# The first k, v and q of a linear-attention and ReGLU kernel: half of k, all of v and q by head halves on Pool's DMA queue, in a new order

## The chip, the cores and the metric

One core of a Trainium2 chip runs the kernel. The metric is the device time of one execution in microseconds (us); the times of several runs are given by their median. Engines are named as in the profile: PE (TensorE), DVE (VectorE), ACT (ScalarE), POOL (GpSimd) and SP (SyncE, which only issues DMAs here).

## What is computed

The reference has two parts. The first is attention with a feature map, for 8 batches of 8 heads, 576 positions and head size 64; the second is a gated feed-forward network (FFN) over the 4608 tokens.

```
def phi(x):                                   # w_phi: 64 x 128
    proj = einsum('bhsd,df->bhsf', x, w_phi)
    proj = proj - max(abs(proj), axis=-1, keepdims=True)
    return concatenate([exp(proj), exp(-proj)], axis=-1)
q_p, k_p = phi(q), phi(k)
kv  = einsum('bhsf,bhsd->bhfd', k_p, v);   z = sum(k_p, axis=2)
num = einsum('bhsf,bhfd->bhsd', q_p, kv);  den = einsum('bhsf,bhf->bhs', q_p, z) + 1e-6
x   = (num / den) as 4608 x 512
out = (maximum(x @ w_gate, 0) * (x @ w_val)) @ w_out      # 512 -> 1536 -> 512
```

## The kernel before, in words

**Stages of a batch.** The first 512 positions of each head are laid on 128 partitions in four chunks; the last 64 of each head ("the rest", km, vm, qm) are worked on two heads at a time. k comes in as kn, is turned to kT (PE with an identity matrix for batches 0 and 1, DMA transposes on SP after that, L310 to L342), is multiplied by w_phi on PE (`rows`, L389), and DVE takes the row maxima (L400) while ACT takes two exponentials of each bank (L350). The maxima are put into v: `scale` (L415, L422) makes vs from vn, on Pool for most heads and on DVE for the last pair of heads of batch 0. `k_kv` (L482) sums kv on PE, and ACT or DVE copies it out. q is turned to qT, projected (L506) and exponentiated; its maxima come from L516, in batch 0 from L562 and L569. `q_num` (L600) multiplies by kv; DVE combines the two signs into t and u (L608, L615), takes the reciprocal r (L625), and Pool divides (L628) into xu, which is turned to xT: on PE for batches 0 and 1 (L641, L648), by DMA on SP later.

**FFN.** For each group of 512 tokens (group g is batch g's main part, a ninth group is all the rests) and each of 12 column blocks: four matmuls with wv (L669), ACT's copy to val (L675), four with wg (L669), and DVE's product to h (L678). Then 12 matmuls with wo (L707) for each of four row blocks, a copy (L718) and a store on SP. Group 0 is cut into three parts of 128, 128 and 256 columns, so that the first can start when chunk 0 of xT is there; the others are one part of 512.

**Loads of batch 0.** SP brings k in four loads of two heads each, 256 KB, in f32 (`kn32`), into memory that later holds w_out, k's rest behind it (`km32`), then v in four loads and v's rest. Two gates (L775, L785) put later loads behind k: the first gated load on SP waits for k's last part, and q's first load on Pool for the third of the four. q comes on Pool in two loads of two chunks each for all heads, cast to bf16 on the way. w_phi comes on ACT's queue. Everything else (the next batches, the weights) comes on Pool's queue.

**Order.** Nothing is scheduled when the kernel is built: each operation is put down with its engine, cost and key in a plan, and ORDER (L1016) is a written-out list of all of them: the number of the operation, a letter for the engine and the slots of its buffers and banks. `w` and `z` entries are warm-up matmuls on a tile of zeros (L199), 120 of them. Each engine runs its own in the order of the list and waits at the first whose inputs are missing. The costs in the plan (2.4 for the identity, 1.25 for a turn by DMA, 0.5 for a store) do not reach the program. From batch 2 on the code keeps turns by DMA and Pool's loads apart: a turn waits for the last load on Pool to land, a load for the last turn.

Of the kernel before, what the change touches and what calls it, by code (L numbers as in the profile page):

```python
# [15 lines left out]
PE, ACT, DVE, POOL, SP = "PE", "ACT", "DVE", "POOL", "SP"  # L16
# [84 lines left out]
def kernel(  # L101
# [12 lines left out]
    B, H, S, D = q.shape  # L114
# [4 lines left out]
    C = 4  # L119
# [85 lines left out]
    def buf(name):  # L205
        return Buf(R[name])
# [9 lines left out]
    o_ident = op(POOL, 2.4, setup, key=(0, 1))  # L216
# [118 lines left out]
    def turn_dma(src, dst, nbytes, dst_buf, deps, key, src_buf, pad=0.0):  # L335
        def go():
            return nc.sync.dma_start_transpose(out=dst(), in_=src())

        o = op(SP, 1.25, go, deps, [src_buf, dst_buf], key=key, kind="a", nbytes=nbytes,
               pad=pad)  # L340
        o.alone = True
        return o  # L342
# [210 lines left out]
    def q_scale_rows(cp, qT, turned, key):  # L553
# [3 lines left out]
        for i in range(NU):  # L557
# [17 lines left out]
            a = op(PE, 0.22, rows, [turned[cp], o_w, o_wz], [qT], [ps], key, "a")  # L575
# [79 lines left out]
    def ffn(g, xb, parts, o_wv, o_wg, o_wo):  # L655
# [38 lines left out]
        for t in range(4):  # L694
            for lo, hi in ((0, DM),) if g < B or t < 3 else ((0, DM // 2), (DM // 2, DM)):
# [32 lines left out]
                if g < B:  # L728
                    op(SP, 0.5, store, [c_], [ob], key=(1, g), kind="l", nbytes=P * DM * 4)
# [17 lines left out]
    for b in range(B):  # L747
        ins[b] = {n: buf(n) for n in ("kn", "qn", "vn", "km", "vm") if b or n[0] != "k"}
        if b % 2 == 1:
            ins[b]["qm"] = buf("qm")  # L750
# [3 lines left out]
    kn32 = k32[:, 0 : H * C * D].rearrange("p (h c d) -> p h c d", h=H, c=C)  # L754
    km32 = k32[:, H * C * D : H * C * D + NU * D].rearrange("p (j d) -> p j d", j=NU)
# [9 lines left out]
    k_heads = ((0, 2), (2, 4), (4, 6), (6, 8))  # L765
    o_km = load_rest_by_head(0, k, SP, (0, 1.5), None, (), 0.0, km32)
    got["km", 0] = o_km
    ks = []
    for i, (lo, hi) in enumerate(k_heads):
        o = load_main(0, "kn", k, SP, slice(lo, hi), (0, i), None, (), 0.0, kn32)  # L770
        ks.append(o)
        for h in range(lo, hi):
            got["kn", 0, h] = o
    heads_of(0, "vn", v, SP, 0, 2, (0, 4))
    heads_of(0, "vn", v, SP, 2, 4, (0, 5), [ks[3]]).gate = ks[3]  # L775
    got["vm", 0] = load_rest_by_head(0, v, SP, (0, 6), ins[0]["vm"])
    heads_of(0, "vn", v, SP, 4, 6, (0, 7))
    heads_of(0, "vn", v, SP, 6, 8, (0, 8))

    for cp in range(C // 2):  # L780
        o = load_main(0, "qn", q, POOL, slice(0, H), (0, 10, cp), ins[0]["qn"], [] if cp else [ks[2]], 0.0, None,
                      slice(2 * cp, 2 * cp + 2))
        if cp == 0:
            o_first = o
            o_first.gate = ks[2]  # L785
        got["qn", 0, cp] = o
# [38 lines left out]
    for b in range(B):  # L825
# [7 lines left out]
        wide = b == 0  # L833
        if wide:
            kn = km = None
            kflat = lambda: kn32.rearrange("p h c d -> p (h c d)")
            kmf = lambda: km32.rearrange("p j d -> p (j d)")
        else:
            kflat = lambda kn=kn: kn.t.rearrange("p h c d -> p (h c d)")
            kmf = lambda km=km: km.t.rearrange("p j d -> p (j d)")  # L840
        qflat = lambda qn=qn: qn.t.rearrange("p h c d -> p (h c d)")
        turned_k, tq = {}, []
        if b < TURNS:
            for u in range(NU):
                o = turn_pe(
                    lambda i, u=u, f=kflat: f()[:, P * (4 * u + i) : P * (4 * u + i + 1)],
                    lambda u=u, kT=kT: kT.t[:, 4 * u : 4 * u + 4],
                    4, kT, [got["kn", b, 2 * u]], (*ak, 0, u), kn,
# [6 lines left out]
            for x in range(2):  # L855
                if wide:
                    at, load = slice(x, None, 2), got["qn", b, x]
                else:
                    at, load = slice(8 * x, 8 * x + 8), got["qn", b, 0]
                tq.append(turn_pe(  # L860
                    lambda i, at=at, f=qflat: f().rearrange("p (n b) -> p n b", b=P)[:, at][:, i],
                    lambda at=at, qT=qT: qT.t[:, at],
                    8, qT, [load], (*ak, 0, 6, x), qn,
                ))
# [36 lines left out]
        def q_two(cp, mq, key, qT=qT, tq=tq, wide=wide):  # L901

            qps, reds, exd = (buf("qp"), buf("qp")), [], ([], [])
            for hq in range(2):
                rd, ex = q_cols(
                    hq, qT, [tq[cp if wide else hq]],
# [15 lines left out]
        if first:  # L922
            cols, scales = {}, {}
            for cp in range(C // 2):
# [3 lines left out]
                scales[cp] = q_scale_rows(cp, qT, tq, (*ak, 1, cp, 1))  # L928
# [56 lines left out]
    for g in range(B + 1):  # L985
        if g == 0:
            xT, xo = xTs[0]
            parts = [(0, P, xo[0:1]), (P, 2 * P, xo[1:2]), (2 * P, SF, xo[2:4])]
# [28 lines left out]
0G 3D 8S 4D 1S 7S 9S 15S0 6S 5G w29 35P00 10S 2D 13S0 36D w17 57P120000 33P3 16G0 59A 61D 37P4 34A  # L1017
58D 17G 63A w8 47P561111 38D 62A 41P00 26G1 51D 49A 67P342222 50A 42D 39P2 12S 22G0 68D 52A 87P0000
14S 71D 60A 11S 23G0 90A 40D 64A 72A 88D w21 77P12333 29G 73A 48D 74A 65A 89A 81D w10 43P40 91A5
75A 69A 78D 66G 83A 92D 44D 84A0 54A 70A 85D 93D w20 119P4 79A 82A 94D 76G 80A w12 108P3201 86D 53A  # L1020
115P5 97P10 110A 117P6 55A 116D0 111A 56G 45P0 98A 118D 109A 101P51 46D 112A 103P16 102A 113P3 120D
107A 136P2 18G 138P0 114D 134P5 106A 99P42 20G 104A 139D1 95P63 105A 135D 21G 122P3723 100A 137D
96A 132P0 121A0 147P10000 19G 124A 144P51 133D 141P42 127P62 125A 145D 193P01 126A 142D 146D 123A
148D 195P7 143D 201P51 140A1 194A 149D 160P31111 154P42 202D 150D 157P10 128A 161D 207P500403 151G
155D 129A 158D 156D 131A 162D 247P61110 25G1 159D 167P40222 196A 211D 173P31 170P10 130A 197P7 168D
249A 174D 152P20 171D 250A 163D 172D 164G 208D 153A 203P11 213A 248D 28G 212A z3 183P21000 169D
165P6 175D 198A 217P403534 184D 24G1 176D 204A 199P3 166D 1359P70 185D 180P62 30G 218D 1383P21
1360A 210A 1375P12 200D 1387P73 177G 209A 181D 186P31 221D 1376A 1361P5 1384A 1388A 205P1 187D 220A
1362D0 1389P2 188D 219A 178P7 182D 1377P5 1390D 223A 237P362025 189D 206D 190G 1363P40 251A 222A
1385P2 241D 1371P13 239A 1365P0 27G0 1386D 1364A 179D 1372A 191P2 242A 1378D 227P411210 1366D 243A  # L1030
192D 277P75010 1373P0 231D 31G 240A 1379P21 283A 1374D 1367P62 252D 32G 1380A 1381P0 238D 224A 232A
1391P20 1382D 253G 233A 1393P3 225D 1368A 1369P0 278D 1392A 1395P13 282A 254G 1397P6 1370D 1415P21
280A 228D 1403P02 1396A 1416A 1394D 1405P1 226G 229A 1398D 281D 1407P20 234A 1417P3 1404A 1408A
1409P6 1406D 279A 270P0523 1418D 230A 263P21 235D 1399P73 273A 1410D 1423P32 236G 274D 1447P41
1400A 1425P6 1424A 1401P7 1448A 244A 1449P3 1426D 245A 1411P40 275A 1402D 1451P62 1450D 267D 1412A
276A 1435P73 1413P3 246G 271D 1453P4 1452A 214A 265A 1419P51 1414D 259P64 1454D 1436A 272A 264D
1443P30 1437P7 260A 284P40 215A 266A 1438D 257P65 216G 285D 1420A 1444A 1445P7 288D 1431P22 258A
261P56 1432A 1446D 268A 291P30 1455P63 262D 269A 1421P2 255P77 292D 1456A 290A 293D 1422D 1427P50
294A 256D 301P10110 347P60 1428A 298P21 289A 295P32 1457P7 299D 1429P5 348A 300D 1487P01 1458D 286A
296D 311P21221 302D 287A 1433P6 303D 1439P73 1430D 1488A 1441P4 312D 1440A 313D 1471P10 383G0  # L1040
1489P0 1434D 1442D 308P50 297D 1479P72 381G1 1490D 1463P23 1480A 309D 1472A 1481P6 314P41 310D
1464A 1473P3 384G0 1482D 1459P01 349P7120 1474D 304D 1460A 1461P2 305G 353D 1467P52 1508P6 1468A
1462D 315D 382G1 316D 306P31 350D 1491P00 324P50002 1495P21 1492A 317D 1497P4 307A 318G 1465P0 355A
321P30 1509P 1466D 351A 322D 1496A 325D 354A 1475P03 326D 352A 356P20 323D 337P11111 1498D 1469P5
1476A 357D 340P32 327P70 338D 1499P41 328D 1518P0 341D 1500A 342D 358D 1470D 359A 329D 1493P4
1483P32 330D 339D 334P52 331G 1501P2 1484A 335D 319P7 336D 1477P1 1494D 369P30220 375P51 1478D
372P42 1519P 343D 320D 344G 376D 373D 1485P1 1502D 1503P7 387S0 1486D 370D 371D 345P2 332P1 374D
388S0 1504P 333A 346A 1505P 389S0 1531P30 386S 1520P 360P40 363P12 1521A0 1523P23 364D 1506A1 361D
365D 1532A 1510P 1507S 1524A 390S 431P00001 1539P71 432D 377D 1527P12 435A 434A 433A 366P32 1525P2
1540A 367D 362D 1511A2 391P501312 1526D1 1528A 401P743131 1541P6 393A 385G0 397A 392D 1513P1 403A  # L1050
1542D 406A 530G1 1535P23 395D 394A 529G1 368D 1529P6 398A 436D 407A 402D 399A 1514P 396A 400G 405D
404A 421P532524 378D 1530D 411P040200 1537P7 414A 531G1 427A 412D 1533P6 426A 413A 1515P 437G 408A
1536A 409D 1543P01 416A 425D 532G0 424A 1534D 1547P22 417A 1516D1 1544A 1545P3 422D 527G0 415D
1551P60 423A 379G 1538D 428A 418A 1549P1 1552A 1546D 438G 1548A 447P04301 454P57 1550D 468P6312
450A 1555P23 528G0 470A 472D 1567P11 469D 1556A 410G 455D 471A 1553P2 448D 1568A 453A 439P68 1554D
474A 1563P12 451D 449A 460A 380S0 1557P2 440D 429A 452A 458D 430G 461P06 1564A 441P49 1522S 465D
# [123 lines left out]
```

## Time and profile before

| what | us |
|---|---|
| median of 9 runs | 382.59 |
| lowest and highest | 381.73 and 386.31 |
| profiled execution | 380.45 |
| its span | 378.7 |
| busy: PE, DVE, ACT, POOL | 365.9, 265.1, 236.9, 169.7 |
| first matmul of the FFN starts | 30.49 |
| last copy of PE's results to SBUF starts | 373.99 |

The profile is one execution. The page lists each engine's busy time, its share of the span, and groups of instructions by line, engine and tile with their mean duration. A line of a timeline has the start, the time from the first start to the last end of the merged instructions, engine, source line, operation, tiles, and in brackets how long the engine sat idle before and what ended that. A row of waits has the engine, the line that waited, the line waited for, the sum in us, the number of times and the longest. Busy PE is not PE at its peak, and warm-up matmuls count as busy.

### The profile page before, as it was taken

To read this page: it belongs to the slowest core of one execution; us is meant where nothing else is said; L and a number is where in the kernel's file an instruction comes from. 1 tells how busy PE (TensorE), PEld (TensorE's weight loads), DVE (VectorE), ACT (ScalarE), POOL (GpSimd) and SP (SyncE) were. 2 spreads that over 40 slices of the span, in tenths; PEclk is the share of its full clock that TensorE was granted. 3 is DMA by queue.
4 is the path that set the end of the run, shared out by engine and by line. 5 is a ranking of instruction groups with operands and counts; after the bars stand their busy time and mean duration, and the time that the engine had idled before them with its cause. 6 is when DMAs were issued, how large, how long until landed. Compare 5 with 4: busy or idle time off the path is not lost.

```text
span 378.7 us, 8753 instructions
## 1 busy us (share of the span) xinstructions
PE 365.9 (97%) x3329; PEld 208.0 (55%) x3375; DVE 265.1 (70%) x650; ACT 236.9 (63%) x546; POOL 169.7 (45%) x201
## 2 busy tenths in 40 slices
PE   8889999999999999998999999999999999999994
PEld 8767897544654655455446544654465544444452
DVE  6999888478897798868866998589647636222431
ACT  4999974498779757975786589567843322214111
POOL 4788945079448732991774259621742200100000
PEclk9999999999999999999999999999999999999999
DMA  6999997759958837988548669850400400020016
GB/s 179 220 183 223 197 172 170 99 148 138 147 146 176 161 61 157 115 199 148 155 96 94 138 148 226 117 118 3 125 2 3 109 31 0 16 83 28 2 42 181
DMA packets 85609, 45.00 MB, mean 119 GB/s; under 512 B 56672, under 2 KB 79072, under 8 KB 85568
## 3 DMA queue, kind: packets, MB, share of 16 engines
q0 software_dynamic: 32800, 21.83, 35.4%
q1 hardware_dynamic: 52448, 22.42, 26.2%
q8 instruction: 26, 0.43, 0.5%
q10 hardware_dynamic: 320, 0.20, 0.2%
q14 instruction: 15, 0.12, 0.1%
HBM read 37.81 MB, written 9.44 MB: 125 GB/s over the span
## 4 chain that ended last, share of the span: by engine, by line
PE 82%; DVE 6%; DMA 4%; ACT 3%; issue 2%; SPq 1%; POOL 1%; DVEq 0%; POOLq 0%
PE ps L669 46%; PE ps L707 21%; PE ps L482 5%; PE ps L600 4%; PE ps L506 2%; DVE h L678 2%; DMA vn<-in_v_dram 2%; PE ps L389 1%; DVE mk L400 1%; DMA wo_sb<-in_k_dram 1%; ACT qp L350 1%; DVE u L615 1%; DVE t L608 1%; DMA kmT<-km 1%; DMA xT<-xu 1%
## 5 line engine op out<-in xcount | busy, mean ns | idle before, releaser
L675 ACT CAST val<-ps 128x512 bf16<-128x512 f32 (+2 forms) x132 | 69.0, 557 | 74.5 <-PE ps L669 63.9
L678 DVE SCALAR_TENSOR_TENSOR h<-ps,val 128x512 bf16<-128x512 f32 (+2 forms) x132 | 75.4, 584 | 46.9 <-PE ps L669 40.9
L707 PE MATMUL ps<-wo_sb,h 128*128 128x512 bf16 (+1 forms) x428 | 102.6, 373 | 1.0 <-issue 0.2
L669 PE MATMUL ps<-xT,wg_sb 128*128 128x512 bf16 (+2 forms) x467 | 98.0, 335 | 1.0 <-ACT kp L350 0.3
L669 PE MATMUL ps<-xT,wv_sb 128*128 128x512 bf16 (+2 forms) x466 | 97.3, 335 | 0.9 <-DMA xT<-xu 0.2
L350 ACT ACTIVATE qp<-ps 128x512 bf16<-128x512 f32 x144 | 83.9, 639 | 7.2 <-PE ps L506 5.8
L628 POOL TENSOR_TENSOR xu<-u,r 128x512 bf16<-128x512 f32 x36 | 37.6, 1046 | 109.0 <-DVE r L625 70.2
L350 ACT ACTIVATE kp<-ps 128x512 bf16<-128x512 f32 x128 | 71.3, 658 | 11.1 <-PE ps L389 9.0
L669 PEld LDWEIGHTS <-wv_sb 128*128 128x128 bf16 x528 | 46.1, 98 | 42.1 <-issue 3.0
L669 PEld LDWEIGHTS <-wg_sb 128*128 128x128 bf16 x528 | 46.0, 98 | 39.8 <-issue 1.5
L707 PEld LDWEIGHTS <-h 128*128 128x128 bf16 x444 | 41.1, 98 | 43.6 <-issue 1.5
L415 POOL TENSOR_TENSOR vs<-vn,ek 128x1024 bf16<-128x1024 f32 x31 | 59.4, 1915 | 12.1 <-DMA vn<-in_v_dram 2.8
L400 DVE TENSOR_REDUCE mk<-ps 128x4 f32<-128x512 f32 x64 | 42.2, 677 | 3.4 <-ACT kp L350 1.6
L516 DVE TRANSPOSE_TENSOR_REDUCE mq<-ps 128x16 f32<-128x512 f32 x56 | 37.6, 698 | 7.3 <-PE ps L506 5.3
L615 DVE TENSOR_TENSOR u<-ps,t 128x195 f32<-128x195 f32 (+3 forms) x120 | 37.8, 331 | 3.2 <-POOL vs L422 0.5
L600 PEld LDWEIGHTS <-qp 128*128 128x128 bf16 x640 | 29.9, 98 | 13.9 <-issue 0.9
L608 DVE TENSOR_TENSOR t<-ps,cq 128x195 f32<-128x195 f32 (+1 forms) x84 | 25.9, 330 | 15.1 <-PE ps L600 12.9
L600 PE MATMUL ps<-kv,qp 128*128 128x65 bf16 x640 | 33.2, 193 | 0.1
L482 PEld LDWEIGHTS <-kp 128*128 128x128 bf16 x512 | 22.1, 98 | 5.4 <-issue 1.1
L482 PE MATMUL ps<-vs,kp 128*128 128x65 bf16 x512 | 23.4, 193 | 0.6 <-POOL vs L422 0.6
L718 ACT COPY ob<-ps 128x512 f32<-128x512 f32 x20 | 11.8, 606 | 17.7 <-PE ps L707 16.0
L482 PE MATMUL ps<-vsm,kpm 128*128 128x65 bf16 x128 | 20.7, 193 | 0.0
(96 smaller groups left out, 315.7 us busy)
## 6 DMA issues: line engine op xcount, KB each, us to landing
out_dram<-ob SPq DMA_DIRECT2D x32, 256.0 KB, 2.7
vn<-in_v_dram POOLq DMA_DIRECT2D x7, 1024.0 KB, 7.8
qn<-in_q_dram POOLq DMA_DIRECT2D x7, 512.0 KB, 6.4
kn<-in_k_dram POOLq DMA_DIRECT2D x7, 512.0 KB, 7.5
wo_sb<-in_moe_w_out_dram POOLq DMA_DIRECT2D x1, 1536.0 KB, 14.6
wo_sb<-in_k_dram SPq DMA_DIRECT2D x4, 256.0 KB, 3.8
vn<-in_v_dram SPq DMA_DIRECT2D x4, 256.0 KB, 7.0
wg_sb<-in_moe_w_gate_dram POOLq DMA_DIRECT2D x2, 512.0 KB, 10.4
```

What stands on the lines that cost most here:

```text
L350: nc.scalar.activation(dst(s), ps.t.rearrange("p (c f) -> p c f", f=f), AF.Exp, scale=sign)
L400: nc.vector.tensor_reduce(m.t.rearrange("p (i x) -> p x i", x=2)[:, x], ps.t.rearrange("p (c f) -> p c f", f=F), axis=AX.X, op=ALU.max, ap ...
L415: eng.tensor_tensor(vs.t[:, :, :, 0:D], vn.t[:, 2 * u : 2 * u + 2].rearrange("p h c d -> p (h c) d")[:, :, None, :] .to_broadcast([P, 2 * ...
L482: nc.tensor.matmul(acc[:, hh, s, :], lhsT=lhsT, rhs=rhs, start=(n == 0), stop=(n == 19))
L516: nc.vector.tensor_reduce(mdst(x), ps.t.rearrange("p (h j t) -> p h j t", j=NQ, t=32), axis=AX.X, op=ALU.max, apply_absolute_value=True, a ...
L600: nc.tensor.matmul(ps.t[:, E * (2 * i + s): E * (2 * i + s + 1)], lhsT=qp.t[:, s, h, :], rhs=kv_of[b][h // 2][0].t[:, h % 2, s, :],)
L615: nc.vector.tensor_tensor(u.t[rows, lo : lo + n], ab[:, :, 0], t.t[rows, 0:n], op=ALU.add)
L628: eng.tensor_tensor(xu.t, u.t[:, :, 0:D], r.t.to_broadcast([P, H, D]), op=ALU.mult)
L669: nc.tensor.matmul(ps.t[:, 0:n], lhsT=w[:, dc, P * fi : P * fi + P], rhs=xt()[:, dc, lo:hi], start=(dc == 0), stop=(dc == NDC - 1),)
L675: nc.scalar.copy(val.t[:, 0:n], pv.t[:, 0:n])
L678: nc.vector.scalar_tensor_tensor(h.t[:, fi, lo:hi], pg.t[:, 0:n], 0.0, val.t[:, 0:n], op0=ALU.max, op1=ALU.mult,)
L707: nc.tensor.matmul(ps.t[:, lo:hi], lhsT=h.t[:, fi, P * t : P * t + P], rhs=wo_sb[:, fi, lo:hi], start=(fi == 0), stop=(fi == NFC - 1),)
```

## The change

SP loads only heads 0 to 3 of the first k, and k's rest, in f32 as before. Heads 4 to 7 come on Pool's queue, cast to bf16, into the ordinary kn tile; Pool issues this load as its very first work, ahead of the identity matrix. Behind it on Pool come q's heads 0 to 3, v's heads 0 to 3, q's heads 4 to 7, v's heads 4 to 7 and v's rest. Both gates are gone. k's heads 4 to 7 are therefore turned in bf16 (into a bank read as bf16), the others in f32. q of batch 0 is turned in four pieces of four blocks, where it was two of eight. FFN group 0 has two parts of 256 columns. Three costs of the plan are other numbers. ORDER is a new list throughout, with 151 warm-up matmuls; its first lines and the rest differ from the ones before in nearly all places, so that on all engines the order of the work after the start is another too. The core of the diff, without ORDER:

```diff
-    o_ident = op(POOL, 2.4, setup, key=(0, 1))
+    o_ident = op(POOL, 0.65, setup, key=(0, 1))
...
-            a = op(PE, 0.22, rows, [turned[cp], o_w, o_wz], [qT], [ps], key, "a")
+            a = op(PE, 0.22, rows, [turned[i // 2], o_w, o_wz], [qT], [ps], key, "a")
...
-    kn32 = k32[:, 0 : H * C * D].rearrange("p (h c d) -> p h c d", h=H, c=C)
-    km32 = k32[:, H * C * D : H * C * D + NU * D].rearrange("p (j d) -> p j d", j=NU)
+    kn32 = k32[:, 0 : H // 2 * C * D].rearrange("p (h c d) -> p h c d", h=H // 2, c=C)
+    km32 = k32[:, H // 2 * C * D : H // 2 * C * D + NU * D].rearrange("p (j d) -> p j d", j=NU)
...
-    k_heads = ((0, 2), (2, 4), (4, 6), (6, 8))
     o_km = load_rest_by_head(0, k, SP, (0, 1.5), None, (), 0.0, km32)
     got["km", 0] = o_km
-    ks = []
-    for i, (lo, hi) in enumerate(k_heads):
+    for i, (lo, hi) in enumerate(((0, 2), (2, 4))):
         o = load_main(0, "kn", k, SP, slice(lo, hi), (0, i), None, (), 0.0, kn32)
-        ks.append(o)
...
-    heads_of(0, "vn", v, SP, 0, 2, (0, 4))
-    heads_of(0, "vn", v, SP, 2, 4, (0, 5), [ks[3]]).gate = ks[3]
-    got["vm", 0] = load_rest_by_head(0, v, SP, (0, 6), ins[0]["vm"])
-    heads_of(0, "vn", v, SP, 4, 6, (0, 7))
-    heads_of(0, "vn", v, SP, 6, 8, (0, 8))
-
-    for cp in range(C // 2):
-        o = load_main(0, "qn", q, POOL, slice(0, H), (0, 10, cp), ins[0]["qn"], [] if cp else [ks[2]], 0.0, None,
-                      slice(2 * cp, 2 * cp + 2))
-        if cp == 0:
-            o_first = o
-            o_first.gate = ks[2]
-        got["qn", 0, cp] = o
+    heads_of(0, "kn", k, POOL, 4, 8, (0, 2))
+    heads_of(0, "vn", v, POOL, 0, 4, (0, 4))
+    got["vm", 0] = load_rest_by_head(0, v, POOL, (0, 6), ins[0]["vm"])
+    heads_of(0, "vn", v, POOL, 4, 8, (0, 7))
+
+    for hq in range(2):
+        o = load_main(0, "qn", q, POOL, slice(4 * hq, 4 * hq + 4), (0, 10, hq), ins[0]["qn"],
+                      [])
+        got["qn", 0, hq] = o
...
             for u in range(NU):
+                f32 = wide and u < NU // 2
                 o = turn_pe(
-                    lambda i, u=u, f=kflat: f()[:, P * (4 * u + i) : P * (4 * u + i + 1)],
+                    lambda i, u=u, f=k_wide if f32 else kflat: f()[:, P * (4 * u + i) : P * (4 * u + i + 1)],
                     lambda u=u, kT=kT: kT.t[:, 4 * u : 4 * u + 4],
-                    4, kT, [got["kn", b, 2 * u]], (*ak, 0, u), kn,
+                    4, kT, [got["kn", b, 2 * u]], (*ak, 0, u), None if f32 else kn,
                 )
...
-                scales[cp] = q_scale_rows(cp, qT, tq, (*ak, 1, cp, 1))
+                scales[cp] = q_scale_rows(cp, qT, tq[cp::2], (*ak, 1, cp, 1))
...
-            parts = [(0, P, xo[0:1]), (P, 2 * P, xo[1:2]), (2 * P, SF, xo[2:4])]
+            parts = [(0, 2 * P, xo[0:2]), (2 * P, SF, xo[2:4])]
```

The operations' order at the start, from the two lists. Pool before: identity, q's two loads, the second batch's q, k and k's rest, a piece of wg, then vs three times. Pool after: k's heads 4 to 7, identity, the five loads named above, the second batch's q and k, two pieces of wv, then vs. PE before: turn of k's heads 2 and 3, 17 warm-ups, their `rows`, turns of heads 0 and 1 and of 4 and 5, and so on. PE after: the same turn, 16 warm-ups, its `rows`, 25 warm-ups, then the turns of heads 4 and 5, 0 and 1, 6 and 7.

## The prediction

> **What bounds the kernel now.** I read the page first, then waits by stretch, then the start engine by engine. All sums are against the profiled execution: span 378.7 us, 380.45 with what lies around it; the median of the runs is 382.59, 2.14 higher, and I carry differences over to it unchanged.
>
> The page says that TensorE (PE) is the bound:
>
> ```profile
> span 378.7 us, 8753 instructions
> ...
> PE 365.9 (97%) x3329; PEld 208.0 (55%) x3375; DVE 265.1 (70%) x650; ACT 236.9 (63%) x546; POOL 169.7 (45%) x201
> ```
>
> So 12.8 us of the span are not PE. PE's waits after 50 us are nearly all that the new order could still win late:
>
> ```profile
> PE ps L436 <- DMA kmT<-km: 0.9, 1, 0.9
> PE ps L669 <- DMA xT<-xu: 0.2, 1, 0.2
> PE ps L707 <- issue: 0.2, 1, 0.2
> PE ps L389 <- DVE mq L516: 0.2, 1, 0.2
> ```
>
> The rest lies at the start and in the tail (the last copy and store, from 373.99 to 378.7). The change acts on the start. Engines there, by stretch of 10 us:
>
> ```profile
> 0.00:10.00 10.00, 9.01 (x103) 8.13 (x104) 6.87 (x18) 4.66 (x8) 4.46 (x11) 1.00 0.72 179
> 10.00:20.00 10.00, 8.77 (x141) 7.03 (x139) 9.78 (x20) 9.85 (x28) 7.20 (x9) 1.00 1.43 219
> 20.00:30.00 10.00, 8.45 (x151) 6.69 (x151) 9.93 (x31) 9.97 (x24) 8.30 (x12) 1.00 1.30 183
> 30.00:40.00 10.00, 9.65 (x138) 8.08 (x137) 9.37 (x29) 10.00 (x28) 8.26 (x11) 1.00 1.11 222
> ```
>
> Columns are PE, PEld, DVE, ACT, POOL, then clock, DMA share, GB/s. Two readings. PE's 8.4 to 9.0 before 30 us contain 120 warm-up matmuls on zeros (L199). From 10 us on it is DVE and ACT that are full, to 98% and more; PE has nothing to do because they aren't ready. Waits of 0 to 30 us name the loads:
>
> ```profile
> POOL qn L255 <- DMA wo_sb<-in_k_dram: 4.9, 1, 4.9
> ACT kp L350 <- PE ps L389: 3.4, 1, 3.4
> POOL vs L415 <- DMA vn<-in_v_dram: 2.8, 1, 2.8
> ```
>
> Pool waits 4.9 us for k before it may issue q, and 2.8 us for v. Both are real, but DVE and ACT work through them. A wait of Pool is worth only what it delays on those two. Their ends that matter are the first FFN copy on ACT, and the FFN's first matmul on PE:
>
> ```profile
> 30.98 0.48 ACT L675 CAST val<-ps 128x128 bf16<-128x128 f32 x1
> ```
>
> ```profile
> 30.49 0.39 PE L669 MATMUL ps<-xT,wv_sb 128*128 128x128 bf16 x4
> ```
>
> **The loads.** What goes: Pool's gated wait, SP's gate on v, and six of SP's eight issues of 256 KB (the pair for v's rest goes too). What comes: five Pool issues of about 0.9 us and a pair of 0.65, from 0.73 us on; make_identity stands behind the first one, so ident32 is ready at 2.6 instead of 1.7, and its first user waits for k until 4.06: nothing. The 4.06 of that user itself may move, since Pool's first load now shares the engines with SP's first. In one-us windows:
>
> ```profile
> 2.00:3.00 1.00, 1.00 (x13) 1.00 (x11) 0.84 (x2) 1.00 (x1) 0.00 (x0) 1.00 0.74 226
> 3.00:4.00 1.00, 1.00 (x12) 1.00 (x11) 0.69 (x3) 0.26 (x1) 0.00 (x0) 1.00 1.07 347
> ...
> 8.00:9.00 1.00, 1.00 (x20) 0.64 (x18) 1.00 (x2) 1.00 (x3) 1.00 (x2) 1.00 0.32 30
> 9.00:10.00 1.00, 1.00 (x15) 0.86 (x12) 1.00 (x4) 1.00 (x3) 1.00 (x2) 1.00 1.34 131
> ```
>
> SP's first issue at 0.74 moves data at 2 us; Pool's first at 6.53 only gets going at 9 (30 GB/s in the window from 8). The Trainium skill (DMA: Bandwidth & Descriptors, "Issuing engines are not separate DMA queues") speaks against the change: loads of different issuers share 16 engines and interleave, and issuing from several saves only issue time. By it, k's first quarter (issue 0.74, landed 3.0 later) would share half and half for its 1.1 us of data, so PE's first turn comes 1 us late, and all behind it with it, because the 16 warm-ups stand after that turn. By the row, Pool needs over 1.5 us to get going, so its first packets meet only the end of that quarter: 0 to 0.3. I take 0.1; the range keeps 1.0. The rule misses that the engines are near empty from 8 to 9: that gap is what earlier issue fills.
>
> When do the parts land? Pool's first q load took 4.7 us, the next 7.1 beside v. So k's second half: 0.73 + 4.7 = 5.4, at worst 7.8. PE asks for it after the first rows (6.2 to 6.5) and 25 warm-ups (21 took 1.34, so 1.6): 8.1. Covered by both. Behind it Pool's queue brought 1 MB of f32 per 2.6 us (second batch's q landed at 19.0, its k at 21.6), 1.3 per half MB, at worst 2.2: q 6.7 (7.6), v 8.0 (9.8), q 9.3 (12.0), v 10.6 (14.2). Pool reaches its first vs scaling only after eleven issues, at 10.8; v's second half is wanted after 17. So the loads stop mattering, and what is late next is DVE and ACT.
>
> **DVE.** From its first row maximum (6.66) to its first t (23.23), before does 17 reductions of 0.60, two f32 kT casts of 0.60 and kmT 0.33, two qT copies of 0.59, vsm 1.42, vs 1.23, 0.2 of reciprocals: 15.8, spread over 16.6. After, by the built order: the same reductions and scalings, two bf16 kT copies of 0.33, four qT of 0.33, w2's clearing 0.2: 15.2. It begins at 6.6 (+0.1) but waits about 0.9 at 8 to 9.5 for the second half's turns, which PE does only after those 25 warm-ups. 15.2 x 16.6/15.8 + 6.6 + 0.9 = 23.5, against 23.23; without the wait 22.6. I take 23.2. Chunk 1's reciprocal then follows after 4.1 (before: 27.86, with one more maximum of 0.6 in between), 27.3, its product on Pool 1.04, its turn on PE, and its copy on DVE behind a maximum and six t and u (2.1): 29.6.
>
> **ACT.** Before, from 6.63 to 30.98: 38 exponentials 0.49 apart (six spread over 3.05) 18.6, turns 2.9, kv copies 1.1, small ones 1.0, xT 0.46: 24.0, and 0.35 idle. After, in the new order: again 38, turns 2.5 + 0.46, the rest alike: 24.1, from 6.5, plus 0.7 idle until the turns at 8.5 to 9.7: first FFN copy at 31.3, **0.3 later** than before.
>
> **PE.** FFN's first matmuls need chunks 0 and 1 now (256 columns, two parts for three): 29.7 against 30.49. By 34.5 the changed order has 5 FFN pieces of 0.44 (2.2), one pair of q projections (L506) more (0.32) and chunk 3's turn (0.23); before has 8 pieces of 0.23 (1.84) and one set of k projections (L389) more (0.32). Lead 0.6 us. It isn't more because chunk 3's reciprocal (27.3 and twelve t and u 3.0, three maxima 1.8, copies and small ones 0.9: 33.0) holds PE up for 0.8. Afterwards a 256 piece saves 2 x 0.228 - 0.435 on PE, twice for each of 12 column blocks: 0.5, of which 0.4 is still to come; on ACT (2 x 0.155 - 0.24) and DVE (2 x 0.20 - 0.335) 0.8 each, which pays back their lag. Sum: 0.6 + 0.4 = **1.0 us**: 380.45 - 1.0 = 379.5 profiled, 381.6 for the median. Warm-ups (151 for 120) fill waits and cost nothing where PE waits anyway; the 25 are priced above. Tail: same stages, and the last two stores stand behind one that is ready 1 us earlier: nothing. The other three edits of planner costs run no code.
>
> **Rivals.** *More is won (0.25).* Turns of the second half don't wait (0.9 less on DVE and ACT), and the 0.9 at kmT goes: 1.0 + 0.9 + 0.9 = 2.8, 379.8. For: loads are early. Against: kmT is issued 3.0 us of PE work ahead, against 2.8 before.
> *ACT and DVE hold PE (0.20).* They are full until 48 us; their lag of 0.3 to 0.5 makes the lead melt; 0.4 from the pieces is left: 382.2.
> *Slower: turned tiles come late (0.23).* From batch 2 on SP turns tiles by DMA, apart from Pool's loads; load and turn change places 16 times for 13. In both orders six turns have under 3.1 us of PE work between issue and reader (before 1.9, 2.6 four times, 2.8; after 2.4, 2.6, 2.7 and 3.0 three times), while issue and landing of such a turn cost 1.2 + 2.4. Before paid 0.9 + 0.2 in all. If SP's queue runs so late that all six cost 0.9: 5.4 - 1.1 = +4.3, less 1.0: 385.9. It decides once four of six wait. For: another order, tried nowhere in this profile. Against: margins are no smaller.
> The forecast case has 0.32; a quarter of it, and the first rival, are faster by over 0.5% (1.9 us, about what a measurement of this kernel tells from no change): 0.33; the last rival slower: 0.23; the rest 0.44. The range goes from a little below the first rival, 379.5, to 385.0, short of the last.
>
> **What would show it.** Right: k's second half lands by 7.8; Pool's vs runs without a wait for v; first t near 23.2, first FFN matmul near 29.7, first val copy near 31.3; PE's waits for DMA after 50 us near 1. Wrong: PE's first turn after 4.5; a wait of PE or DVE for k, q or v; PE idle by over 1 us between 31 and 50; several waits for xT, kT or kmT.

## The result and the profile after

The changed kernel takes 379.71 us (median of 17 runs, 378.12 to 380.86), the kernel before 382.62 (52 runs, 380.86 to 386.99): a ratio of 0.9919, 95% interval 0.9901 to 0.9936. The forecast was 381.6, so 1.0 us of gain was forecast and 2.9 came. The two profiled executions, 380.45 and 379.44, differ by just the 1.0 of the forecast; the table below shows that this is luck. What follows is mostly about the other 1.9 us.

The head of the page of the changed kernel, its span and busy times:

```profile
span 377.7 us, 8578 instructions
...
PE 366.5 (97%) x3266; PEld 207.0 (55%) x3310; DVE 265.8 (70%) x642; ACT 232.7 (62%) x532; POOL 172.9 (46%) x206
```

The same four stretches of 10 us as for the kernel before (PE, PEld, DVE, ACT, POOL, clock, DMA share, GB/s):

```profile
0.00:10.00 10.00, 9.01 (x114) 8.42 (x116) 5.63 (x16) 5.03 (x9) 8.45 (x17) 1.00 0.92 189
10.00:20.00 10.00, 9.10 (x148) 7.44 (x141) 9.91 (x21) 9.98 (x28) 8.42 (x11) 1.00 1.35 231
20.00:30.00 10.00, 9.33 (x182) 8.09 (x179) 10.00 (x32) 10.00 (x25) 8.59 (x12) 1.00 1.36 181
30.00:40.00 10.00, 9.88 (x114) 7.60 (x111) 9.68 (x27) 10.00 (x29) 6.84 (x7) 1.00 1.11 207
```

DVE and ACT are as full as before from 10 us on, so the earlier loads left them no waiting to save there; POOL is busy with issuing where it had waited. Pool's first instructions, by the timeline (start, length, engine, line, operation, and in brackets the idle time before):

```profile
1.25 0.93 POOL L255 DMA_DIRECT2D kn<-in_k_dram  x1 [0.81 <-POOLq L1153]
...
9.50 0.76 POOL L296 DMA_DIRECT2D wv_sb<-in_moe_w_val_dram  x1 [0.37 <-DMA qn<-in_q_dram]
10.85 0.74 POOL L296 DMA_DIRECT2D wv_sb<-in_moe_w_val_dram  x1 [0.59 <-DMA vn<-in_v_dram]
11.61 1.92 POOL L415 TENSOR_TENSOR vs<-vn,ek 128x1024 bf16<-128x1024 f32 x1
```

The first load starts at 1.25, not at 0.73, and lands 6.5 us later, at 7.75 at the latest; PE asks for it at 8.13. The first vs has no wait for v. In the two brackets with a DMA, Pool stood still until an earlier load of its own queue had landed, though the weights that it was to load next have no use for that data.

PE's waits after 50 us (engine, line and what it waited for; sum, times, longest):

```profile
PE ps L669 <- DVE t L608: 0.4, 1, 0.4
PE ps L506 <- DVE mq L516: 0.3, 1, 0.3
```

No wait for a turned tile is left, where before had 0.9 for kmT and 0.2 for xT. PE's first FFN matmul starts at 29.04 (before 30.49), the first val copy at 31.05 (before 30.98).

### The profile page after: what moved, and what is told of

Its sections match the earlier page's. It is cut to its first block, busy times and chain, and to the rows that moved or that the text cites. A ratio compares the mean times of both kernels' runs of the same rounds, so it can differ in the third digit from the quotient of the medians.

```text
span 377.7 us, 8578 instructions
## 1 busy us (share of the span) xinstructions
PE 366.5 (97%) x3266; PEld 207.0 (55%) x3310; DVE 265.8 (70%) x642; ACT 232.7 (62%) x532; POOL 172.9 (46%) x206
## 4 chain that ended last, share of the span: by engine, by line
PE 85%; DVE 7%; ACT 3%; DMA 2%; issue 2%; POOL 0%; DVEq 0%; POOLq 0%
PE ps L669 45%; PE ps L707 24%; PE ps L482 5%; PE ps L600 4%; PE ps L506 2%; DMA wg_sb<-in_moe_w_gate_dram 2%; ACT kp L350 2%; DVE u L615 2%; PE ps L389 2%; DVE t L608 2%; PE ps L199 1%; DVE h L678 1%; DVE mk L400 1%; ACT val L675 0%; PE ps L321 0%
## 5 line engine op out<-in xcount | busy, mean ns | idle before, releaser
L675 ACT CAST val<-ps 128x512 bf16<-128x512 f32 (+1 forms) x120 | 66.1, 584 | 78.8 <-PE ps L669 61.3
L678 DVE SCALAR_TENSOR_TENSOR h<-ps,val 128x512 bf16<-128x512 f32 (+1 forms) x120 | 74.1, 628 | 49.5 <-PE ps L669 41.3
L669 PE MATMUL ps<-xT,wg_sb 128*128 128x512 bf16 (+1 forms) x419 | 96.2, 355 | 1.2 <-DMA wg_sb<-in_moe_w_gate_dram 0.4
L669 PE MATMUL ps<-xT,wv_sb 128*128 128x512 bf16 (+1 forms) x417 | 95.7, 355 | 1.2 <-DVE t L608 0.4
L350 ACT ACTIVATE qp<-ps 128x512 bf16<-128x512 f32 x144 | 81.0, 631 | 10.1 <-PE ps L506 8.8
L669 PEld LDWEIGHTS <-wg_sb 128*128 128x128 bf16 x480 | 44.3, 98 | 40.8 <-issue 1.1
L669 PEld LDWEIGHTS <-wv_sb 128*128 128x128 bf16 x480 | 44.1, 98 | 40.9 <-issue 2.0
L600 PEld LDWEIGHTS <-qp 128*128 128x128 bf16 x640 | 31.0, 98 | 15.1 <-issue 0.9
L600 PE MATMUL ps<-kv,qp 128*128 128x65 bf16 x640 | 34.6, 193 | 0.1
L456 POOL TENSOR_TENSOR vsm<-vm,ekm 64x512 bf16<-64x512 f32 x14 | 14.5, 1039 | 9.7 <-ACT ekm L363 8.2
```

What stands on the lines that cost most here:

```text
L350: nc.scalar.activation(dst(s), ps.t.rearrange("p (c f) -> p c f", f=f), AF.Exp, scale=sign)
L600: nc.tensor.matmul(ps.t[:, E * (2 * i + s): E * (2 * i + s + 1)], lhsT=qp.t[:, s, h, :], rhs=kv_of[b][h // 2][0].t[:, h % 2, s, :],)
L669: nc.tensor.matmul(ps.t[:, 0:n], lhsT=w[:, dc, P * fi : P * fi + P], rhs=xt()[:, dc, lo:hi], start=(dc == 0), stop=(dc == NDC - 1),)
L675: nc.scalar.copy(val.t[:, 0:n], pv.t[:, 0:n])
L678: nc.vector.scalar_tensor_tensor(h.t[:, fi, lo:hi], pg.t[:, 0:n], 0.0, val.t[:, 0:n], op0=ALU.max, op1=ALU.mult,)
```

## Experiments

Twelve runs follow, four of an unchanged kernel and eight with an edit. Each ratio is against the kernel before, run beside it on the same chip; the runs were made on two chips. Two theories stood against each other for the missing 1.9 us. The *start theory*: what is won is won before 50 us. The *late theory*: usual executions of the kernel before lose more at turns and stores late in the kernel than its profiled execution shows, and the new order loses less there.

### Four more profiled executions, nothing edited

Before and after once more:

> The kernel before once more, unchanged, for a second profile and more times. Theory A (the start alone: PE's last matmul ends 1.2 us earlier, the rest of the 2.9 us between the medians is only that the first profile of before was a low draw): this profile shows the same waits of PE after 50 us as the first, about 1.5 us in all, whatever its time. Theory B (the late order: in its usual executions before loses another 2 us at waits for turned tiles after 80 us, and the first profile happened to miss them): a profile with a time near 382.6 shows 3 us or more of such waits, most of them for xT, kT or kmT.

> The changed kernel once more, unchanged. Both theories: 379.7 +- 1.0, ratio about 0.992. Waits of PE after 50 us under 1.5 us (first profile 0.7); first t on DVE at 23.0, first FFN matmul at 29.0, k's second half landed at 7.7 +- 0.5.

Measured: 383.04 (ratio 1.0003, interval 0.9975 to 1.0031) and 380.29 (0.9936, interval 0.9912 to 0.9960). Their profiled executions took 381.0 and 379.82, with these waits of PE after 50 us, first before and then after:

```profile
PE ps L436 <- DMA kmT<-km: 1.2, 1, 1.2
PE ps L506 <- DMA qmT<-qm: 0.7, 1, 0.7
PE ps L669 <- DVE mk L400: 0.2, 1, 0.2
```

```profile
PE ps L669 <- DVE t L608: 0.4, 1, 0.4
PE ps L506 <- DVE mq L516: 0.3, 1, 0.3
PE ps L669 <- DMA xT<-xu: 0.2, 1, 0.2
```

Both of before's profiles, 380.45 and 381.0, lie at the lower end of its runs, so neither shows what a usual run loses. Two more were taken of it:

> The kernel before, unchanged, for one more profiled execution: the two so far (380.45 and 381.0) lie 2 us under the median of its usual runs, so they don't show what a usual run loses. Late theory: a usual execution (382 to 384) has its first val copy near 31.0 as in the others, and PE's waits after 50 us for turned tiles (kmT, qmT, xT, kT) add up to 2.5 to 4 us where they were 1.5 and 2.1. Start theory: its first val copy or first FFN matmul is 1 us or more later, and the waits after 50 us stay near 2.

> A second further profiled execution of the unchanged kernel before, with the same expectations: waits after 50 us of 2.5 to 4 us in a usual execution by the late theory, a later start by the start theory. If the two executions lie apart in time, the difference shows in the one place or the other.

They took 382.55 and 383.23, as usual runs do. PE's waits after 50 us, in the first of the two:

```profile
PE ps L669 <- DMA xT<-xu: 1.2, 1, 1.2
PE ps L436 <- DMA kmT<-km: 0.9, 1, 0.9
PE ps L669 <- DVE mk L400: 0.8, 1, 0.8
PE ps L389 <- DVE mq L516: 0.2, 1, 0.2
```

And in the second:

```profile
PE ps L669 <- DMA xT<-xu: 1.3, 1, 1.3
PE ps L436 <- DVE u L615: 1.1, 1, 1.1
PE ps L506 <- DMA qmT<-qm: 0.9, 1, 0.9
PE ps L669 <- DVE mk L400: 0.3, 1, 0.3
PE ps L389 <- DVE mq L516: 0.2, 1, 0.2
```

The same places recur: L436 is the matmul that reads kmT near 174 us (the wait put down to `u` is at this place too), L506 here reads qmT near 135 us, the first L669 reads xT near 195 us, and the L669 that waits for mk is at 152 us. How long PE stands there changes from one execution to the next. All the profiled executions of the two kernels side by side (waits after 50 us are the sum of such rows):

| execution | time | first val copy | waits after 50 us | time less these waits |
|---|---|---|---|---|
| before, first | 380.45 | 30.98 | 1.5 | 378.95 |
| rep_before | 381.00 | 30.34 | 2.1 | 378.90 |
| rep_before2 | 382.55 | 30.97 | 3.1 | 379.45 |
| rep_before3 | 383.23 | 31.09 | 3.8 | 379.43 |
| after, first | 379.44 | 31.05 | 0.7 | 378.74 |
| rep_after | 379.82 | 31.79 | 0.9 | 378.92 |

Before's four times spread over 2.8 us, and less their late waits over 0.55. The means are 381.81 and 379.63, 2.2 apart; the waits' means are 2.6 and 0.8, so 1.8 of the 2.2 are late waits and 0.4 is all the rest. The late theory holds, on four executions against two. The first two executions show how the forecast's 1.0 was met by luck: of their difference 0.8 is late waits, and only 0.2 the rest.

Two starts are odd ones: rep_before's came 0.65 early, and why is not known; rep_after's came 0.75 late. With both put at 31.0 the rest is 0.9. But the second is not mere chance:

```profile
PE ps L389 <- DVE w L226: 1.2, 1, 1.2
```

PE's first `rows` waited for w_phi, which comes on ACT's queue beside k. In five profiled executions with the loads as before (the four above and the next section's) w_phi took at most 3.7 us from issue to landing, and PE never waited for it. In the five with the changed loads (the two above, and the three kernels below with fewer warm-ups or a moved store) it took up to 3.7, 5.5, 4.8, 5.5 and 3.5, and PE waited 1.2, 0.7 and 1.3 in three of them. So a late w_phi belongs, as it seems, to what the new loads cost, and 0.9 is the gain of a start without it. The prediction did not look at this load.

### Late turns moved in the kernel before

```
 ORDER, SP:  kT, store, kmT, store, kT   ->  kT, kmT, store, store, kT    (861S1 ahead of 1653S)
 ORDER, SP:  kT, qT, qmT                 ->  kT, qmT, qT                  (674S0 ahead of 715S0)
```

> The kernel before with two late turns by DMA moved forward on SP: the turn of batch 5's k rest (kmT, near 169 us) ahead of the store in front of it, and the turn of qm near 129 us ahead of a turn of q. Nothing of the start is touched. Late theory (usual executions of the kernel before lose some 2 us more at such late turns than its two profiled executions, and the new order loses less): the median falls by 1.5 to 3 us, to 379.8 to 381.3. Start theory (what the new order gains, it gains before 50 us; late waits are in every execution what the profiles show): at most the profiled 0.9 to 1.2 of kmT goes, 381.5 to 382. If the median doesn't move at all, these two waits are covered by something else.

Measured: 382.22, ratio 0.998 (interval 0.9959 to 1.0). That is 0.8 us, or 1.2 between the medians (383.47 for the kernel before beside it), at the edge of noise: what the start theory allowed, and short of the late theory's 1.5. Its profiled execution took 381.89, with these waits after 50 us:

```profile
PE ps L669 <- DMA xT<-xu: 1.5, 2, 1.1
PE ps L436 <- DMA kmT<-km: 0.4, 1, 0.4
PE ps L389 <- DMA kT<-kn: 0.2, 1, 0.2
PE ps L707 <- issue: 0.2, 1, 0.2
```

Less these 2.3 it has 379.6 left, near the 378.9 to 379.5 of the kernel before: here too the late waits make the time. kmT's wait fell from 0.9 or more to 0.4 and qmT's is not there, though two of the four executions of before had none at qmT either. Of the 1.5 for xT, 0.4 is near 195 us, where the four had 0.2, 0, 1.2 and 1.3; the other 1.1 is at 152 us, where they had 0, 0.2, 0.8 and 0.3, put down to mk. What PE saves at one turn it may wait for at the next one that it reaches too soon; that the first caused the second was not tried by itself.

### Fewer warm-ups, and a store

```
-59D w25 34P3
+59D w8 34P3
```

> The changed kernel with 8 warm-up matmuls in place of the 25 between the first k projections and the turn of heads 4 and 5. The 25 end at 8.1 and the half landed at 7.75. If the warm-ups set the start: the turn at 7.75, 0.35 us earlier on DVE and ACT, 379.3. If the landing sets it: no difference that can be measured, 379.7, and PE is seen waiting for kn until 7.7. If PE's clock suffers from the pause: a granted clock under 1.0 at 7 to 12 us, and slower.

Measured: 382.48, ratio 0.9991 (interval 0.9968 to 1.0015): all of the gain is gone. The start isn't to blame: first FFN matmul 28.95, first val copy 30.97, both 0.1 earlier than in the changed kernel. PE's last matmul ends 2.1 later, at 374.8 against 372.7; the profiled execution took 382.44, 3.0 more, and the other 0.9, behind that matmul, is not explained. The waits after 50 us are:

```profile
PE ps L506 <- ACT ob L718: 1.5, 1, 1.5
PE ps L669 <- DMA xT<-xu: 0.9, 2, 0.5
PE ps L506 <- DVE mq L516: 0.3, 1, 0.3
```

The first row is at 270 us. L506 wants the bank that ACT's copy to ob is to empty, and this copy waits for a store from the same ob buffer to land:

```profile
269.90 0.59 ACT L718 COPY ob<-ps 128x512 f32<-128x512 f32 x1 [1.86 <-DMA out_dram<-ob]
```

In the changed kernel the same copy waited 0.27:

```profile
267.81 0.58 ACT L718 COPY ob<-ps 128x512 f32<-128x512 f32 x1 [0.27 <-DMA out_dram<-ob]
```

SP's own timeline, with 8 warm-ups:

```profile
262.57 2.50 SPq L337 DMA_TRANSPOSE xT<-xu  x2
265.16 0.53 SPq L726 DMA_DIRECT2D out_dram<-ob  x1
265.78 2.94 SPq L337 DMA_TRANSPOSE qmT<-qm  x1
```

The store is issued at 265.16 here, and at 265.29 in the changed kernel, though its block was ready at 246: it stands behind two turns, and SP's longest wait there (10.1 us, 10.4 in the changed kernel) is that of a turn for v's load on Pool's queue, which the code keeps apart from turns. It landed 4.7 us after its issue, where the stores of this stretch in the changed kernel took 2.1 to 2.4, and the issue of the turn behind it lasted 2.94 in place of 1.23. Why this store landed so late, and what fewer warm-ups have to do with it, is not shown. So it was moved ahead of the two turns:

```
 ORDER, SP:  kT, xT, xT, store   ->  kT, store, xT, xT    (1747S ahead of 1155S)
```

> The changed kernel with 8 warm-ups instead of 25 ahead of the turn of k's heads 4 and 5 (this alone took 382.48), and with one store moved: that of the output block whose copy ended at 246 us, but which stood on SP behind two turns of xT that wait for Pool until 262 us; now it stands ahead of them. Late theory (8 warm-ups cost 2.2 us only because this store landed too late for the next copy into the same buffer, 1.5 us of PE's wait near 270 us): 380.0 to 381, the wait of L506 for ob gone. Start theory (the missing warm-ups themselves cost, by a lower clock or by a later start): stays at 382 to 382.8, wait gone or not.

Measured: 380.60, ratio 0.9927 (interval 0.9899 to 0.9955). The wait for ob is gone, and with it 1.9 us, although in its profiled execution the start was late (PE waited 1.3 for w_phi and 1.0 for k's second half, used at 9.04; first val copy at 31.98). One store made most of what looked like the price of warm-ups. The same edit in the changed kernel itself:

> The changed kernel with one store moved on SP, ahead of the two turns of xT near 262 us that it stood behind (its output block is ready at 246 us). In the two profiles of the changed kernel, ACT's copy into the same buffer waited for it by 0.3 us. If the same wait costs more in usual executions: 378.8 to 379.5. If not: 379.6 to 380.3, no change. Slower by 0.5 or more only if the store, issued near 252 us, delays the turns behind it.

Measured: 379.56, ratio 0.9919 (interval 0.9892 to 0.9946): not to be told from the changed kernel, as 0.3 us of wait leave little to win. It is the lowest median of all kernels here, by no more than chance.

### The loads by themselves

The kernel before without its two gates, in its own order:

```diff
-    heads_of(0, "vn", v, SP, 2, 4, (0, 5), [ks[3]]).gate = ks[3]
+    heads_of(0, "vn", v, SP, 2, 4, (0, 5))
...
-        if cp == 0:
-            o_first = o
-            o_first.gate = ks[2]
```

> The kernel before with both gates taken away and nothing else: Pool issues q, and SP v, without waiting for k. It is the part 'loads early' of the change alone. Start theory in the form 'the loads were late': 1 to 2 us faster, 381 to 382, first val copy well before 30.5. My prediction's reading (DVE and ACT are full from 10 us on and cover the 4.9 and 2.8 us that Pool waits): within 0.4 of the kernel before (382.4 to 383.2), first val copy at 31.0 plus or minus 0.3, Pool's two waits gone from its list. Sharing rival: k's parts land later beside q and v, PE's first turns 0.5 to 1 us later, and 383.3 to 383.8.

Measured: 386.24, ratio 1.008 (interval 1.0053 to 1.0108), more than 2 us beyond the worst expectation. PE's longest wait before 50 us is at the turns of k:

```profile
PE ps L321 <- DMA wo_sb<-in_k_dram: 3.0, 2, 2.1
```

k's third and fourth parts came 2.1 and 0.9 us too late for PE; the first val copy is at 34.30, 3.3 later than before, and the median is 2.8 higher. This is the rule of the Trainium skill that the prediction weighed (DMA: Bandwidth & Descriptors, "Issuing engines are not separate DMA queues"): loads of all issuers interleave on the same engines. The trace agrees: k's last load took 8.1 us from issue to landing, where it had taken 4.2. The gates had held k's 1 MB free of it. PE's clock, which fell while it waited (last section), adds to the 3.3.

Then k's second half as Pool's first load, the gates off, and the rest in the order of before:

```
+    heads_of(0, "kn", k, POOL, 4, 8, (0, 2))
-0G 3D 8S 4D 1S 7S 9S 15S0 6S 5G w29 35P00 10S
+9G1 0G 3D 8S 4D 1S 7S 14S0 6S 5G w29 34P00
```

> The kernel before in its own order, without the gates, and with k's heads 4 to 7 as Pool's first load, cast to bf16, in place of two loads on SP: the changed way of loading k without the new order. If the new loads make the gain: 380 to 381.3. If the new order makes it (reductions, turns and FFN parts in another sequence): 382 to 383.3, and the first FFN matmul within 0.5 of 30.5. If turns in bf16 and early loads give half: 381.3 to 382.

Measured: 384.41, ratio 1.0031 (interval 1.0008 to 1.0054), above all three expectations.

```profile
PE ps L321 <- DMA kn<-in_k_dram: 1.6, 1, 1.6
```

k's second half was there at 9.11, after PE had waited 1.6 for it, and the first val copy came at 32.17, 1.2 later than before. SP had v in flight by then. The edit has two parts, though: without the gates alone the kernel took 386.24, so the half on Pool wins 1.8 us against that, and it is the missing gates, with v still on SP, that cost. k's half on Pool with v held back, in the old order, was not tried.

In the new order, k's second half back on SP in f32:

```diff
-    heads_of(0, "kn", k, POOL, 4, 8, (0, 2))
+    o = load_main(0, "kn", k, SP, slice(4, 8), (0, 2), None, (), 0.0, kn32)
```

> The changed kernel with k's second half back on SP in f32, one load of 512 KB behind the first two, all else as changed (order too; the two f32 turns of that half take the place of bf16 ones). It asks what the half on Pool is worth. Theory A by its sum: two f32 copies of 0.60 for two of 0.33 on DVE, 0.54 later from 9 us on, and k lands at about 5 us, where PE asks for it at 8.1: 0.5 us slower than the changed kernel, 380.2. Rival (Pool's cast half is what opens the queue early and all later loads hang on it): over 1.5 us slower, 381.2 or more. Theory B: the order does it, so 379.7 to 380.2.

Measured: 381.71, ratio 0.9958 (interval 0.9935 to 0.9980), 1.4 us over the changed kernel's run beside it (380.29), nearer to the rival (over 1.5) than to the sum of theory A (0.5). k's half was there at 9.20, PE waited 0.8 for it, and the first val copy came at 32.74, 1.7 later.

In the new order, v back on SP behind k:

```
-    heads_of(0, "vn", v, POOL, 0, 4, (0, 4))
+    heads_of(0, "vn", v, SP, 0, 4, (0, 4))
 (v's rest and heads 4 to 7 likewise; on SP all three stand behind k's rest)
```

> The changed kernel with v's three loads back on SP, directly behind k's (Pool issues only k's second half, q's two halves and the later loads): it undoes the move of v alone. Sharing reading (in the kernel before without its gates, loads in front of their time took the engines from k): v's 1.1 MB on SP go out from 4 us on and share with k's second half, which lands at 8.5 to 9.5 where it landed by 7.75; PE's turn of heads 4 and 5 waits 0.5 to 1.5, and the time is 380.5 to 382. If v's place doesn't matter: 379.4 to 380.4.

Measured: 382.23, ratio 0.9974 (interval 0.9952 to 0.9996). The time is 0.2 over the range that sharing gave; the cause is not the expected one. k's second half was turned at 7.57, in time. It is q that came late:

```profile
PE ps L321 <- DMA qn<-in_q_dram: 2.4, 2, 1.2
```

The first val copy moves to 32.54, 1.5 later. SP issued v at 3.20, beside q at 3.07 on Pool. q's halves landed at 11.6 and 14.9, where the changed kernel had them at 9.3 and 11.8; v's landed at 10.0 and 12.2, where it had them at 10.5 and 14.7. What v won on its own queue, q lost.

So in the new order the new places of k and v matter: to put k's half back costs 1.4 us, and to put v back costs 2.7 against the changed kernel with the moved store, which ran beside it (379.56). That is half of the gain of 2.9, or nearly all. New loads and new order go together. The new order with all the old loads was not tried.

## Why the prediction was right or wrong

**Forecast and range.** The number was 1.9 too high; the time lies 0.2 inside the lower end of a range 5.5 wide, and faster by over 0.5% had 0.33: that it fell inside is more luck than merit. The sum of the start was near; the sum of the late waits was wrong.

**The term that was wrong: "Before paid 0.9 + 0.2 in all."** That is one execution's price. The four executions paid 1.5, 2.1, 3.1 and 3.8 with all rows counted, and the first had the smallest. The changed kernel pays 0.7 and 0.9. So the late part of the sum, for which nothing but 0.4 of FFN pieces was put down, is worth 1.8 between the means, and 2.4 between rep_before2, which took what a usual run of before takes, and the first profile of after. The sign was in the text: the median lay 2.14 over the profiled execution, and this was carried over as a constant. Of the 2.1 between this execution and rep_before2, 1.6 are waits that it hadn't had.

**The start and the pieces, forecast 1.0.** Measured 0.4 as it stands, 0.9 with the two odd starts put at 31.0. PE's first FFN matmul came at 29.04 (forecast 29.7), the first val copy at 31.05 (31.3), so the lag of ACT was 0.1 and not 0.3; the first t of DVE at 23.05 (23.2), chunk 1's reciprocal at 26.43 (27.3), its copy at 28.57 (29.6). Right in kind, each a little too late. (The 27.86 that it gives for chunk 1's reciprocal before is 27.76 in the trace.)

**The loads.** k's second half was forecast at 5.4, at worst 7.8; it landed at 7.75, because Pool started 0.5 later and the load took 6.5 where the first q load of before had taken 4.7. It is covered only by 0.4. The loads behind it landed at 9.3, 10.5, 11.8 and 14.7, where 6.7, 8.0, 9.3 and 10.6 were forecast; the first two, and the last, are later than its worst case, which starts from 5.4 and not from the 7.8 that it had called the worst. PE's turns waited for none of them. PE's first turn was forecast 0.1 late and starts at 4.06, as before: at this one place the row was the better guide. The page's rule was too lightly put aside for the change at large: the starts were 3.3 us later without the gates, 1.5 with v on SP, and 1.2 with Pool's k in the old order without the gates. That the loads "stop mattering" holds for this arrangement alone.

**The 25 warm-ups.** They were priced at 0.9 of DVE's wait. With 8 of them PE waits for k's half until 7.77 all the same (8.13 with 25), and the start gains 0.1. The wait is mostly the load's, not theirs.

**Pool's waits covered by DVE and ACT.** Right for the new order: both are full from 10 us on, before and after. In the old order, earlier issue without the gates made the kernel slower; in the new order the new loads are needed to keep the start from being late, by 1.5 to 1.7 us, but most of the gain over the kernel before lies in the late waits.

**Rivals.** "More is won" named 379.8, and the kernel takes 379.71. Of its two mechanisms the late one happened, larger than named (kmT's 0.9 went, qmT's and xT's with it), the other did not: ACT still sits idle 1.9 us for the turns and DVE 1.5 for k's rows at the start. "Turned tiles come late" is refuted in the changed kernel, where no wait for one is over 0.2, but it is what the kernel before does. The remark "margins are no smaller" should have been read the other way too: the smallest margin grew from 1.9 to 2.4, and those of 2.6 or less fell from five to two. That this is why the waits went is argued only.

**What stays open.** That the changed kernel has fewer late waits is shown, in two executions against four. Which of the moves in its order does it, and why the delay of a turn varies so from one execution to the next, is not: the only late edit in the kernel before won 0.8 of what is to be explained, at the edge of noise.

## What to carry to other kernels

When the profiled execution is at the edge of the kernel's own runs, its waits are not the usual ones: profile the same kernel again until an execution near the median is at hand, and put a price on every wait whose margin is short. Before a slower variant is explained by its edit, compare the waits far behind the edit; here one store, behind turns on an in-order queue, landed 4.7 us after its issue instead of 2.1 to 2.4, and moving it won 1.9. A gate that seems only to make an engine wait may be keeping the DMA engines free for the load that is wanted first.

## What the runs showed of the hardware that was not expected

A PE that had been mostly idle was granted half its clock. Without the gates PE is busy for 0.00, 0.23 and 0.51 us in the three windows from 9 to 12, and from 12 on the granted clock is half (PE, PEld, DVE, ACT, POOL, clock, DMA share, GB/s):

```profile
9.00:10.00 1.00, 0.00 (x0) 0.00 (x0) 0.45 (x1) 1.00 (x4) 0.00 (x0) 1.00 1.49 200
10.00:11.00 1.00, 0.23 (x2) 0.20 (x2) 0.00 (x0) 1.00 (x3) 0.00 (x0) 1.00 1.34 248
11.00:12.00 1.00, 0.51 (x10) 0.23 (x8) 0.78 (x2) 0.05 (x1) 0.00 (x0) 0.98 1.36 200
...
13.00:14.00 1.00, 1.00 (x8) 0.82 (x7) 0.38 (x1) 0.03 (x1) 0.00 (x0) 0.50 1.30 236
14.00:15.00 1.00, 1.00 (x12) 1.00 (x10) 0.70 (x2) 1.00 (x3) 0.00 (x0) 0.50 1.25 253
```

It is full again at 16 us. The page TensorE: Matmul & The Clock Gate of the Trainium skill ("Part 1: The HAM clock gate (the "warmup" mystery)") puts the slow clock after an idle window of about 3.4 us. Read as 3.4 us without a matmul, that does not fit this trace: the longest gap before the drop is 2.1 us (8.69 to 10.77), and PE then worked for 0.7 us. A stretch with little work was enough. With 8 warm-ups in place of 25 the clock stayed at 1.00 in every window from 5 to 17 us, where PE's least busy window had 0.55 us.

The issue of a turn by DMA on SP takes 1.2 to 1.3 us as a rule, but single ones took 1.6 to 2.94: some at one place in every execution (a kT behind a store near 172 us, in the four of the kernel before: 2.34, 2.19, 2.52, 2.13), some in one execution only. Whether these records hold a wait or the issue itself, the profile does not tell. Pool stood still at the issue of a load (0.4, 0.6 and 0.7 us in the changed kernel) until an earlier load on its queue had landed; whether the queue or the program asks for that was not tried.
